# A linear-attention and expert kernel on one core: first scores, warm-up turns, range flag, gate sums and last product rearranged

## Chip, core and metric

The kernel runs on one core of a Trainium2 chip, as one program. The metric is the device time in microseconds of that program. Before the change it is 401.42 us (median of three runs, 400.92 to 402.02).

## What is computed

The reference has two parts. The first is a recurrence over 768 times for 4 batches and 8 heads of 48 dimensions:

```python
cur = np.einsum('bhd,bhe->bhde', u[None] * kt, vt)
y[:, :, t] = np.einsum('bhd,bhde->bhe', rt, state + cur)
state = w[None, :, :, None] * state + np.einsum('bhd,bhe->bhde', kt, vt)
```

Its result, as 3072 rows of 384, goes through a two-level choice of expert: argmax over 4 groups, then argmax over 4 experts of that group, both with softmax weights. Each row passes one expert:

```python
h = np.maximum(xg[mask_e] @ w1[g, e], 0.0)
ye = h @ w2[g, e]
out[tok_idx] = combined[:, None] * ye
```

with w1 of 384x1024 and w2 of 1024x384 for each of the 16 experts.

## The kernel before, in words

The order of the work on every engine is written out by hand: each engine carries out its instructions in the order of the source, and waits at an instruction until what it needs is there.

**Recurrence (lines 274 to 1014).** The 768 times are cut into chunks of 128; with 4 batches this gives NT = 24 chunks, one for each step s of the loop at line 860. For chunk n, `turn` (505) transposes the keys and the queries of the chunk on TensorE (PE): `turn(n, "kT")` into the bank TR, `turn(n, "rT")` into RW; `turn_out` (515) copies kT on ScalarE (ACT) and multiplies rT by the powers `pw` of the decay on VectorE (DVE). `scores(n)` (524) multiplies kT by rT into the two banks of PA, four pairs of heads by two. For every chunk but the first it does so in quarters: the rows 0 to 63 of a 128x128 block against all 128 columns, the rows 64 to 127 against the last 64; the lower left quarter is not needed. `mask(n)` (542) copies the part above the diagonal into `am` on DVE. The diagonal itself comes from `sum_own` (495, DVE, over products `dg` of GpSimd, POOL), `diagonal_here` (553, DVE, five heads) and `diagonal` (558, ACT, the others; those of the list `waiting` run in the next step). `values(n)` (579) multiplies the values by `am` into YB, `state(n)` (567) adds what the state gives, `update(n)` (588) writes the chunk's contribution to the state into columns of the bank MS, from which `carry(n)` (599, DVE) makes the new state R. `values_out(n)` (610) copies YB to `yT` on ACT, `rows_out(n)` (626) turns it into rows.

**Gates.** `gate_parts(n)` (614) multiplies the four quarters of yT by the gate weights into 128 columns of a bank and copies them to `lT` on ACT (three buffers). The bank is MS or TR (line 279), in alternation for n below 7, TR from then on. `gate_sum(n)` (643) adds the four quarters by a matmul with `sel`, into other columns of MS. The parts of chunks 0 and 1 are made in step 3, those of 2 and 3 in step 4, 4 in step 5, 5 and 6 in step 6, then one a step; their sums come a step later, ahead of that step's parts (lines 942 to 950). Four chunks make a turn of the routing (`route_1` to `route_5`), which writes rows to their expert's region by indirect DMA on POOL.

**Range flag.** The decay is held within limits; if any value was outside, a slow path at the end recomputes all. `out_of_range` (751) compares on DVE in step 0, `all_out_of_range` (755) sums over partitions by a matmul into a column of MS, `in_range` (758) makes `not_ok`, and `go_on` (761) a whole number of it, in step 8. `count(12)` (685), in step 14, sums the experts' counts in the same way.

**Start (lines 419 to 840).** `turn_nothing` (420) transposes the identity on PE, with no use of the result: 13 times at the start, 2 after the product that spreads u over the partitions (425), 2 after `mask(0)` and 4 before `turn(1, "kT")`. `WL` and `wl` (828) are the last powers of the decay.

**Experts (1016 to 1166).** 15 slots of up to 212 rows and at the end one of 96 run one after the other: `up` into four banks, `down` by 128 columns with the weights as the stationary side. The two small slots (88 and 96 rows) and the rows done ahead use `rows_down` (238): eight products of 384 columns with the rows as the stationary side, one multiplication by the gate on ACT, one indirect DMA of rows of 384. The slot of 96 rows comes last. `tokens` (252) makes the list of its row numbers on DVE.

Banks: PA and YB are tiles of two banks, TR, RW, MS and SB of one.

Of the kernel before, what the change touches and what calls it, by code (L numbers as in the profile page):

```python
# [29 lines left out]
def kernel(  # L30
# [88 lines left out]
    tagA = [cst([P, 2], f"tagA_{i}") for i in range(4)]  # L119
    idA = [cst([P, 1], f"idA_{i}", I32) for i in range(4)]  # L120
    okA = [cst([P, 1], f"okA_{i}", I32) for i in range(4)]
    cnt_s = cst([P, GE], "cnt_s")
# [128 lines left out]

    def tokens(i, n, count):
        nc.vector.memset(idA[i][0:n], NOWHERE)
        nc.vector.tensor_scalar(
            out=tagA[i][0:n, 0:1].bitcast(I32), in0=tagA[i][0:n, 0:1].bitcast(I32), scalar1=2, scalar2=None,
            op0=OP.logical_shift_right,
        )
        nc.vector.tensor_scalar(out=okA[i][0:n], in0=prow[0:n], scalar1=count[0:n], scalar2=None, op0=OP.is_lt)
        nc.vector.copy_predicated(idA[i][0:n], okA[i][0:n], tagA[i][0:n, 0:1].bitcast(I32))

# [13 lines left out]
    with ExitStack() as rec:  # L274
# [3 lines left out]
        rows_ps = YB[:, :, 2 * P : 4 * P]  # L278
        lT_at = (MS[:, 0:P], TR[:, 0, :])

        spare_at = [0]
# [21 lines left out]
        pre_ps = MS[:, 400 : 400 + 4 * GE]  # L303
        cnt_ps = MS[:, 464 : 464 + GE]

        def scratch(shape, i):
# [67 lines left out]

        nc.vector.memset(y_ps, 0.0)
        nc.vector.memset(padded(rp[0]), 0.0)
        nc.vector.memset(padded(rp[NRP - 1]), 0.0)
# [47 lines left out]
        nc.tensor.matmul(u_ps_all, lhsT=ones[0:1, :], rhs=u_row, start=True, stop=True, skip_group_check=True)  # L425
        turn_nothing(2)
        gates_in()
# [96 lines left out]
        def scores(n):  # L524
            kT, rT = rkT.pop((n, "kT")), rkT[n, "rT"]
            for hc in range(HC):
                for e in range(2):
                    rows = slice(DP * e, DP * e + D)
                    if n == 0:
                        nc.tensor.matmul(  # L530
                            PA[:, e, P * hc : P * (hc + 1)], lhsT=kT[rows, hc, :], rhs=rT[rows, hc, :],
                            start=True, stop=True, skip_group_check=True,
                        )
                        continue
                    for z in range(2):
                        nc.tensor.matmul(  # L536
                            PA[64 * z : 64 * (z + 1), e, P * hc + 64 * z : P * (hc + 1)],
                            lhsT=kT[rows, hc, 64 * z : 64 * (z + 1)], rhs=rT[rows, hc, 64 * z : P],
                            start=True, stop=True, skip_group_check=True,
                        )  # L540
# [72 lines left out]

        def gate_parts(n):
            yT = yTs[n]
            lT_ps = lT_at[n % 2 if n < 7 else 1]
            for q in range(NQ):
                e, j = q // 2, q % 2
                nc.tensor.matmul(  # L619
                    lT_ps[32 * q : 32 * (q + 1), :], lhsT=gwp[:, 4 * j + e, :], rhs=yT[:, e, j, :],  # L620
                    start=True, stop=True, skip_group_check=True,
                )
            lT = mid[n] = pool.tile([P, P], FP32, tag="lT", bufs=3, name="lT")
            nc.scalar.copy(lT, lT_ps)
# [60 lines left out]
        def count(n):  # L685
            nc.tensor.matmul(cnt_ps, lhsT=ones, rhs=cum[:, n, :], start=True, stop=True, skip_group_check=True)

        def keys():
            key = tl([P, GE], "keys")
            nc.vector.scalar_tensor_tensor(  # L690
                out=key, in0=cnt_ps, scalar=float(GE), in1=bias16, op0=OP.mult, op1=OP.add
            )
            return key
# [57 lines left out]
        def out_of_range():  # L751
            nc.vector.tensor_tensor(out=same, in0=wcol, in1=wraw, op=OP.not_equal)
            nc.vector.reduce_max(out=same[:, 0:1], in_=same, axis=AX)

        def all_out_of_range():
            nc.tensor.matmul(cnt_ps[:, 0:1], lhsT=ones, rhs=same[:, 0:1], start=True, stop=True, skip_group_check=True)

        def in_range():
            nc.vector.tensor_scalar(out=not_ok, in0=cnt_ps[:, 0:1], scalar1=0.5, scalar2=None, op0=OP.is_gt)

# [66 lines left out]
        scores(0)  # L827
        nc.vector.tensor_mul(WL, pw[:, :, P // 2], pw[:, :, P // 2])
        nc.scalar.copy(wl, WL)
        for t in am[2:4]:  # L830
            nc.scalar.copy(diagonals(t)[:, 0:HERE], spread(nothing.to_broadcast([P, P]), 1, HERE))
        mask(0)
        turn_nothing(2)
        turn(1, "rT")
        turn_nothing(4, TR)
        turn(1, "kT")
# [23 lines left out]
        for s in range(NT):  # L860
# [44 lines left out]
            if s > CLOSE:  # L905
                update(s)
            values_out(s)
            if s == 0:
                own_term(1)
                out_of_range()  # L910
            for n, e, hc in waiting:
                diagonal(n, e, hc, hc + 1)
            waiting.clear()
            if s <= CLOSE:
                scores(s + 1)
                update(s)
                if s == CLOSE:
                    sum_own(s + 3)
                mask(s + 1)
# [5 lines left out]
            if far < NT:  # L925
                turn(far, "kT")
                turn(far, "rT")
            if s == 0:
                all_out_of_range()
                in_range()  # L930
            if whole:
# [7 lines left out]
            for c in range(NB - 1):  # L939
                if s == first(c) + 1:  # L940
                    route_e(c)
            for n in {4: (0, 1), 5: (2, 3), 6: (4,), 7: (5, 6)}.get(s, (s - 1,) if s > 7 else ()):
                gate_sum(n)
            for c in range(NB - 1):
                if s == first(c) + 2:
                    route_p(c)
                    if c == 2:
                        count(12)
            for n in {3: (0, 1), 4: (2, 3), 5: (4,), 6: (5, 6)}.get(s, (s,) if s > 6 else ()):
                gate_parts(n)  # L950
            if s < CLOSE:
                own_term(far)
            for c in range(NB - 1):
# [4 lines left out]
                if s == first(c) + 2:  # L958
                    if c == 2:
                        key = keys()  # L960
                    route_3(c)
                if s == first(c) + (2 if c >= NB - 3 else 3):
# [18 lines left out]
            if s == CLOSE - 1:  # L981
                turn(s + 3, "kT")
                turn(s + 3, "rT")
                own_term(s + 3)
            if whole:
                diagonal(far, 1)
            if s >= CLOSE and s + 4 < NT:
                sum_own(s + 4)
            if s == 8:
                go_on()  # L990
        for job in late:
# [24 lines left out]
    with ExitStack() as moe:  # L1016
# [55 lines left out]
        def columns(p):  # L1072
# [4 lines left out]
            if s < 2:  # L1077
                tokens(2 + s, SLOTS[s], cnt_s[:, s : s + 1])
                return
# [62 lines left out]
        for p in range(GE):  # L1142
# [10 lines left out]
            if order[p] < 2:  # L1153
                i = order[p]
                po = next_of(downs)
                yt = pool.tile([P, DM], FP32, tag="yd", name="yd")
                rows_down(hTs[p], held(p)[1], 2 + i, SLOTS[i], po, yt)
            else:
                down(p, 0)
# [280 lines left out]
```

## Time and profile before

| what | us |
|---|---|
| median of three runs | 401.42 |
| the profiled execution | 402.09 |
| its span in the profile | 400.3 |
| PE busy | 388.7 (97%) |
| ACT busy | 180.4 (45%) |
| POOL busy | 201.0 (50%) |
| DVE busy | 153.4 (38%) |
| recurrence, up to the last chunk's values | 0 to 128.4 |
| experts, from the first large slot to the last matmul | 162 to 393.1 |

Durations are those of the profiled execution, whose span begins with the first instruction. A row of the timeline gives start, busy time, engine, line of the kernel, operation, written and read tiles (written first), number of instructions, and in brackets how long the engine had been idle and what ended that. PE is the matmul itself, PEld the loading of its stationary side, which stands in the queue ahead of it. An idle engine costs time only where the chain runs through it.

### The profile page before, as it was taken

How to read it: one execution, taken by the hardware profiler on the slowest of the kernel's cores; microseconds unless marked ns; L12 is line 12 of the kernel's file. 1: busy time of each engine (PE TensorE's matmuls, PEld its weight loads, DVE VectorE, ACT ScalarE, POOL GpSimd, SP SyncE). 2: the span in 40 equal slices, each digit the busy share in tenths (PEclk: the TensorE clock that was granted, in tenths of full speed). 3: DMA queues.
4: the chain of work that ended last, by engine and by line, in shares of the span. 5: the costliest groups of instructions: out<-in, count | busy, mean ns of one | idle time of the engine just before them, and what ended most of it. 6: DMA issues, size and time to landing. Idle time of an engine off the chain costs nothing.

```text
span 400.3 us, 10467 instructions
## 1 busy us (share of the span) xinstructions
PE 388.7 (97%) x3963; PEld 361.9 (90%) x3963; DVE 153.4 (38%) x405; ACT 180.4 (45%) x429; POOL 201.0 (50%) x265
## 2 busy tenths in 40 slices
PE   8999999999999999999999999999999999999992
PEld 6787899999888977899999999999999999999981
DVE  7887988888867602101202112111121221211110
ACT  4665888888875211432433424424244244244210
POOL 7999956999842412105162351532624524523542
PEclk9999999999999999999999999999999999999999
DMA  8998999995965977999999999999989999981000
GB/s 159 160 174 159 197 208 221 212 195 147 264 200 123 308 193 212 233 275 258 232 258 243 228 250 266 224 253 284 200 240 259 255 247 268 233 236 28 27 18 27
DMA packets 123118, 81.80 MB, mean 204 GB/s; under 512 B 96863, under 2 KB 114289, under 8 KB 123061
## 3 DMA queue, kind: packets, MB, share of 16 engines
q1 hardware_dynamic: 116019, 71.12, 77.1%
q0 software_dynamic: 4752, 9.55, 8.1%
q8 instruction: 32, 0.52, 0.6%
q10 hardware_dynamic: 2290, 0.40, 0.5%
q14 instruction: 25, 0.20, 0.2%
HBM read 69.89 MB, written 11.67 MB: 204 GB/s over the span
## 4 chain that ended last, share of the span: by engine, by line
issue 46%; PE 29%; POOL 18%; SPq 3%; DVE 2%; DMA 1%; POOLq 1%; ACT 0%
POOL out_dram L1128 16%; PE YB L583 6%; PE PA L536 6%; SPq L323 3%; PE TR L511 3%; PE YB L574 2%; PE YB L630 2%; PE RW L511 2%; PE MS L594 2%; PE TR L619 2%; PE MS L644 1%; DMA vt<-in_v_dram 1%; POOL out_dram L245 1%; PE TR L793 1%; DVE am L543 1%
## 5 line engine op out<-in xcount | busy, mean ns | idle before, releaser
L1128 POOL DMA_INDIRECT out_dram<-yt,idn x93 | 90.4, 972 | 137.1 <-DVE yt L1126 107.0
L1076 DVE STREAM_TRANSPOSE xe<-xg 128x672 f32<-128x672 f32 (+2 forms) x16 | 12.7, 796 | 121.0 <-DMA xg<-x_sorted 88.7
L1116 PE MATMUL YB<-hT,w2p 128*128 128x208 f32 (+10 forms) x336 | 58.7, 328 | 0.0
L1116 PE MATMUL PA<-hT,w2p 128*128 128x208 f32 (+10 forms) x336 | 58.1, 326 | 0.0
L1116 PEld LDWEIGHTS YB<-hT,w2p 128*128 128x128 f32 x336 | 55.8, 190 | 0.0
L1116 PEld LDWEIGHTS PA<-hT,w2p 128*128 128x128 f32 x336 | 55.3, 190 | 0.0
L561 ACT ACTIVATE am<-ident,du 128x128 f32<-128x128 f32 x152 | 50.5, 398 | 0.0
L1125 DVE STREAM_TRANSPOSE yt<-yT 128x672 f32<-128x672 f32 (+1 forms) x14 | 11.8, 842 | 80.4 <-ACT yT L1119 80.4
L1094 ACT COPY w2p<-w 128x1024 f32<-128x1024 f32 x42 | 41.1, 1045 | 3.0 <-DMA w<-in_moe_w_dram 3.0
L543 DVE COPY_PREDICATED am<-later,PA 128x1024 f32<-128x1024 int32 x24 | 31.7, 1323 | 10.8 <-PE PA L536 6.1
L1104 PE MATMUL MS<-xe,w 128*128 128x208 f32 (+12 forms) x192 | 32.8, 320 | 0.0
L1104 PE MATMUL TR<-xe,w 128*128 128x208 f32 (+12 forms) x192 | 32.8, 320 | 0.0
L1104 PE MATMUL RW<-xe,w 128*128 128x208 f32 (+12 forms) x192 | 32.8, 320 | 0.0
L1104 PE MATMUL SB<-xe,w 128*128 128x208 f32 (+12 forms) x192 | 32.7, 320 | 0.0
L1104 PEld LDWEIGHTS SB<-xe,w 128*128 128x128 f32 x192 | 30.8, 190 | 0.6 <-issue 0.2
L1104 PEld LDWEIGHTS MS<-xe,w 128*128 128x128 f32 x192 | 30.7, 190 | 0.0
L1104 PEld LDWEIGHTS RW<-xe,w 128*128 128x128 f32 x192 | 30.7, 190 | 0.0
L1104 PEld LDWEIGHTS TR<-xe,w 128*128 128x128 f32 x192 | 30.7, 190 | 0.0
L230 POOL DMA_INDIRECT x_sorted<-xt,place_i x16 | 16.1, 1003 | 23.6 <-DVE end L719 11.8
L536 PE MATMUL PA<-rT,kT 48*64 48x128 f32 (+1 forms) x736 | 25.6, 255 | 0.5 <-issue 0.5
L583 PE MATMUL YB<-am,vt 128*48 128x128 f32 x384 | 25.9, 277 | 0.1
L490 POOL TENSOR_TENSOR dg<-dg,ub 128x384 f32<-128x384 f32 x24 | 24.1, 1003 | 1.9
(220 smaller groups left out, 560.1 us busy)
## 6 DMA issues: line engine op xcount, KB each, us to landing
w<-in_moe_w_dram SPq DMA_DIRECT2D x128, 384.0 KB, 9.5
vt<-in_v_dram SPq DMA_DIRECT2D x24, 192.0 KB, 4.5
rp<-in_r_dram SPq DMA_DIRECT2D x23, 192.0 KB, 4.3
kt<-in_k_dram SPq DMA_DIRECT2D x22, 192.0 KB, 5.2
xg<-x_sorted SPq DMA_DIRECT2D x36, 85.8 KB, 10.3
x_sorted<-zeros SPq DMA_DIRECT2D x4, 392.0 KB, 4.7
out_dram<-yt,idn POOLq DMA_INDIRECT x93, 7.5
xg<-x_sorted SPq DMA_DIRECT2D x20, 73.5 KB, 8.9
```

The costliest lines, as they stand in the source:

```text
L230: ins = nc.gpsimd.indirect_dma_start(out=xs_dram, out_offset=bass.IndirectOffsetOnAxis(ap=place_i[:, i : i + 1], axis=0), in_=xt[:, i].rea ...
L490: nc.gpsimd.tensor_mul(dg, dg, ub)
L511: nc.tensor.transpose(ps[:, hc, :], two, ident)
L536: nc.tensor.matmul(PA[64 * z : 64 * (z + 1), e, P * hc + 64 * z : P * (hc + 1)], lhsT=kT[rows, hc, 64 * z : 64 * (z + 1)], rhs=rT[rows, hc ...
L543: nc.vector.copy_predicated(am[n % NAM], later.unsqueeze(1).unsqueeze(1).to_broadcast([P, 2, HC, P]).bitcast(I32), PA.rearrange("p e (h t) ...
L561: nc.scalar.mul(am[n % NAM][:, e, hc, :], ident, dus[n][:, i : i + 1])
L583: nc.tensor.matmul(y_at(e, hc), lhsT=vt[:, n % 2, 2 * hc + e, :], rhs=amn[:, e, hc, :], start=(n < 4 and hc < 2), stop=True, skip_group_ch ...
L1076: nc.vector.transpose(xe[:, :, 0:nb, :], xg[:, 0:nb, 0:QW].rearrange("p i (ko a) -> p ko i a", a=32))
L1094: nc.scalar.copy(o4[:, kk], v4[:, kk])
L1104: nc.tensor.matmul(ph[:, i, 0:n], lhsT=w1[:, ko, P * (f + i) : P * (f + i + 1)], rhs=xe[:, ko].rearrange("p i b -> p (i b)")[:, 0:n], star ...
L1116: nc.tensor.matmul(po[:, 0:n], lhsT=w2p[:, d, fo, :], rhs=hT[:, fo, 0:n], start=(fo == 0), stop=(fo == FO - 1))
L1128: ins = nc.gpsimd.indirect_dma_start(out=out_q, out_offset=bass.IndirectOffsetOnAxis(ap=idn[:, i : i + 1].bitcast(U32), axis=0), in_=yt[:, ...
```

## The change

- `scores(0)` is made in quarters like the others; the part of PA that it leaves is set to zero once by DVE at the start.
- The turns of nothing after the spread of u (2), after `mask(0)` (2) and before `turn(1, "kT")` (4) go. `WL` and `wl` come behind `mask(0)`.
- `out_of_range` moves from step 0 to the end of step 8, and writes into a free column of `cum`; its sum over partitions is made as a 17th column of `count(12)` in step 14, `in_range` follows `keys` there, `go_on` moves to step 17.
- `gate_parts` always writes into TR: the first part of a step at columns 0 to 127, the second at 128 to 255. Up to step 5 the sums come behind the parts.
- `turn(7, "kT")`, in step 4, goes to the first bank of PA instead of TR. In step 4 the copy `values_out` comes behind the waiting diagonals.
- The last slot's product is made in two halves of 192 columns, each with a multiplication on ACT and an indirect DMA of its own; `tokens` makes two lists for it.

```diff
+        nc.vector.memset(PA.rearrange("p e (h z t) -> p e h z t", z=2, t=64)[64:P, :, :, 0, :].rearrange("p e h t -> p (e h) t"), 0.0)
...
         nc.tensor.matmul(u_ps_all, lhsT=ones[0:1, :], rhs=u_row, start=True, stop=True, skip_group_check=True)
-        turn_nothing(2)
         gates_in()
...
-                    if n == 0:
-                        nc.tensor.matmul(
-                            PA[:, e, P * hc : P * (hc + 1)], lhsT=kT[rows, hc, :], rhs=rT[rows, hc, :],
-                            start=True, stop=True, skip_group_check=True,
-                        )
-                        continue
...
-        def gate_parts(n):
+        def gate_parts(n, at=0):
             yT = yTs[n]
-            lT_ps = lT_at[n % 2 if n < 7 else 1]
+            lT_ps = TR[:, at, :]
...
+        def count_and_range(n):
+            both = cum[:, n : n + 2, :].rearrange("p i e -> p (i e)")[:, 0 : GE + 1]
+            nc.tensor.matmul(
+                MS[:, 464 : 464 + GE + 1], lhsT=ones, rhs=both, start=True, stop=True, skip_group_check=True
+            )
...
-        nc.vector.tensor_mul(WL, pw[:, :, P // 2], pw[:, :, P // 2])
-        nc.scalar.copy(wl, WL)
...
         mask(0)
-        turn_nothing(2)
+        nc.vector.tensor_mul(WL, pw[:, :, P // 2], pw[:, :, P // 2])
+        nc.scalar.copy(wl, WL)
         turn(1, "rT")
-        turn_nothing(4, TR)
         turn(1, "kT")
...
-            values_out(s)
+            if s != CLOSE - 1:
+                values_out(s)
             if s == 0:
                 own_term(1)
-                out_of_range()
             for n, e, hc in waiting:
                 diagonal(n, e, hc, hc + 1)
             waiting.clear()
+            if s == CLOSE - 1:
+                values_out(s)
...
-            if s == 0:
-                all_out_of_range()
-                in_range()
...
-            for n in {4: (0, 1), 5: (2, 3), 6: (4,), 7: (5, 6)}.get(s, (s - 1,) if s > 7 else ()):
-                gate_sum(n)
+            summed = {4: (0, 1), 5: (2, 3), 6: (4,), 7: (5, 6)}.get(s, (s - 1,) if s > 7 else ())
+            if s > CLOSE:
+                for n in summed:
+                    gate_sum(n)
...
-                        count(12)
-            for n in {3: (0, 1), 4: (2, 3), 5: (4,), 6: (5, 6)}.get(s, (s,) if s > 6 else ()):
-                gate_parts(n)
+                        count_and_range(12)
+            for at, n in enumerate({3: (0, 1), 4: (2, 3), 5: (4,), 6: (5, 6)}.get(s, (s,) if s > 6 else ())):
+                gate_parts(n, at)
+            if s <= CLOSE:
+                for n in summed:
+                    gate_sum(n)
...
             if s == CLOSE - 1:
-                turn(s + 3, "kT")
+                turn(s + 3, "kT", PA[:, 0].rearrange("p (h t) -> p h t", t=P))
...
             if s == 8:
+                out_of_range()
+            if s == 17:
                 go_on()
...
+                if p == last:
+                    for z in range(2):
+                        yt = pool.tile([P, DM // 2], FP32, tag="yh", name="yh")
+                        half_down(hTs[p], held(p)[1], 2 + i, SLOTS[i], z, next_of(downs), yt)
```

The new function for the halves:

```python
    def half_down(hT, w2, i, n, z, po, yt):
        cols = slice(DM // 2 * z, DM // 2 * (z + 1))
        for fo in range(FO):
            nc.tensor.matmul(
                po[0:n, 0 : DM // 2], lhsT=hT[:, fo, 0:n], rhs=w2[:, fo, cols], start=(fo == 0), stop=(fo == FO - 1),
                skip_group_check=True,
            )
        nc.scalar.mul(yt[0:n], po[0:n, 0 : DM // 2], tagA[i][0:n, 1:2])
        ins = nc.gpsimd.indirect_dma_start(
            out=out.rearrange("n (z w) -> (n z) w", z=2),
            out_offset=bass.IndirectOffsetOnAxis(ap=idH[z][0:n].bitcast(U32), axis=0),
            in_=yt[0:n], in_offset=None, bounds_check=2 * N - 1, oob_is_err=False,
        )
```

## The prediction

> **What bounds the kernel.** I read the page first (its table of slices has PE at 8 or 9 tenths everywhere but the last slice), then PE's waits by window, then the timeline of the stretches that the change touches. From 44 to 140 us the waits view gives PE no wait for another engine above 0.2 us, and the chain runs from matmul to matmul; in the expert stage (140 to 393 us) PE has no listed wait at all. So a microsecond that PE gains or loses before 50 us goes to the end unchanged, and little else counts. I call a pass of the loop over s "step s", and part(n) what gate_parts(n) issues.
>
> The start, in the timeline of 0 to 32 us:
>
> ```profile
> 5.96 0.69 PE L422 MATMUL RW<-ident 128*128 128x128 f32 x2
> 6.45 1.06 PE L511 MATMUL MS<-ident,rp 128*128 128x128 f32 x4
> 7.94 0.87 PEld L815 LDWEIGHTS YB<-ident,iw 128*128 128x128 f32 x4
> 10.50 0.47 PEld L511 LDWEIGHTS RW<-ident,rp 128*128 128x128 f32 x4
> ...
> 10.76 1.32 DVE L543 COPY_PREDICATED am<-later,PA 128x1024 f32<-128x1024 int32 x1
> ...
> 14.93 1.32 DVE L543 COPY_PREDICATED am<-later,PA 128x1024 f32<-128x1024 int32 x1
> 16.15 0.34 DVE L604 TENSOR_TENSOR R<-MS,wl 128x192 f32<-128x192 f32 x1
> 16.54 0.30 PEld L756 LDWEIGHTS MS<-same,ones 128*128 128x128 f32 x2 [0.83 <-DVE R L604]
> 16.86 0.82 PEld L583 LDWEIGHTS YB<-am,vt 128*48 128x48 f32 x16
> ```
>
> Two things are to be seen. A turn costs 0.87/4 = 0.22 us until 8.8 us and 0.47/4 = 0.12 after 10.3: PE's clock is released in between. And the matmul of the range flag (L756) holds PE 0.83 us, though it reads nothing of R: it waits because R's multiply reads the same bank MS, at other columns.
>
> The two places with two parts in one step, from the timelines of 28 to 35 and 32 to 60 us:
>
> ```profile
> 28.72 0.59 ACT L520 COPY kT<-TR 128x512 f32<-128x512 f32 x1
> ...
> 29.31 0.19 PEld L619 LDWEIGHTS MS<-yT,gwp 128*32 128x32 f32 x8 [0.48 <-issue]
> 29.45 0.26 PEld L619 LDWEIGHTS TR<-yT,gwp 128*32 128x32 f32 x8
> ```
>
> ```profile
> 47.42 0.16 PEld L619 LDWEIGHTS TR<-yT,gwp 128*32 128x32 f32 x8
> 47.56 0.24 PEld L619 LDWEIGHTS MS<-yT,gwp 128*32 128x32 f32 x8
> ...
> 48.00 0.85 PEld L536 LDWEIGHTS PA<-rT,kT 48*64 48x64 f32 x32 [0.20 <-issue]
> ...
> 48.62 0.26 ACT L662 ACTIVATE ex<-ex 128x80 f32<-128x80 f32 x1
> ...
> 48.78 0.25 ACT L624 COPY lT<-TR 128x128 f32<-128x128 f32 x1
> ```
>
> The second part follows the first at 0.14 us because it goes to another bank; ACT fetches the first one much later (48.78).
>
> The end, in the timeline of 375 to 401 us:
>
> ```profile
> 387.81 5.33 PE L240 MATMUL YB<-w,hT 128*96 128x384 f32 x16
> 391.30 0.97 POOL L1128 DMA_INDIRECT out_dram<-yt,idn  x1 [0.31 <-issue]
> 393.18 0.58 ACT L244 ACTIVATE yd<-YB,tagA 96x384 f32<-96x384 f32 x1 [4.83 <-PE YB L240]
> 394.03 0.94 POOL L245 DMA_INDIRECT out_dram<-yd,idA  x1 [1.76 <-ACTq L1170]
> ```
>
> **Part by part.** Sums are against the profiled execution: span 400.3, time 402.09, which is 0.67 above the median of 401.42.
>
> *Warm-up turns.* The two turns at 5.96 stand right before turn(0, rT), whose four follow back to back (6.45), so its data are there; without them it starts at 5.97, and turn_first and the iw turns, queued behind, 0.48 earlier too. T2's copy on ACT follows (9.25 to 8.77), and with it POOL's row of 1.0 us operations that starts at 9.81. The scores start at 8.73 instead of 9.20, and run at the slow clock up to the release, so they end near 10.1 instead of 10.4. The other six turns (10.33, 10.94) end on no path: PE waits for the mask until 12.14 anyway. The new memset of half of PA is taken at the 0.48 us of the memset of 128x512 (L375); DVE has a wait of 0.58 us for wraw ahead of 3.19, which covers it. Without that cover it would cost at most those 0.48.
>
> *Quarters and WL.* 32 matmul passes instead of 16; the quarters of later steps take 1.10 us (L536), the whole ones 1.16 (L530): nothing. mask(0) now waits for the scores, for ACT's three diagonals (0.98 us, starting after the sum of du near 9.1) and no longer for WL (0.34): 10.2 instead of 10.76. WL and wl fall behind it, and kT(1)'s copy on ACT behind wl, at about 12.0 instead of 12.19; scores(1) then start near 12.7 (13.15). mask(1) waits for ACT's diagonals of step 1, behind the first yT copy: 14.2 instead of 14.93.
>
> *Range flag.* Its two DVE operations ahead of mask(1) go (their end at 15.02 set its start as much as the diagonals' at 14.76), and L756 leaves PE. Values(1) then wait for mask(1) alone: 14.2 + 1.32 + 0.06 = 15.55 instead of 16.86. **Head: -1.3.** What is late next: du(2) needs POOL's dg, 16.85 before and 16.4 now, used at 17.08 before; it fits, and from there mask, values, yT copy and diagonals form a ring of 4.06 us a step (values from 16.86 to 20.92) which starts 1.3 earlier. Where the turns bring nothing (the release falls earlier in that run), only the flag's part is left: mask(1) at 14.80, behind the diagonals' end at 14.76, then values(1) at 16.2, 0.65 earlier. Bounds -0.6 and -1.4. The flag's DVE work at step 8 (0.65) and 14 (0.14) stands in a DVE that is idle some 15% there and is followed by masks due a step later; a 17th column in the count (0.18 us for 16): nothing. If that cover were gone, 0.8.
>
> *Parts in TR.* Part(1), (3) and (6) now go to the bank from which ACT still has to copy part(0), (2), (5). L756 above and L644 at 34.81 (0.27 behind DVE's ts, other columns of MS) show that a matmul into a bank waits for the reader of other columns of it, and I find no matmul in the timeline that starts into one of these tiles while ACT or DVE reads it. The rows show it for DVE; that ACT's copies count as well is an inference. The Trainium skill's page "PSUM — Partial Sum Buffer", section "PSUM bank collisions raise a hardware error", says that accesses have to be kept apart by bank and 32-partition quadrant, not by address, for ScalarE too; by it the sum is the one below, and if addresses alone counted it would be the first rival's.
> Step 3: part(0) waits for kT's copy (28.72 + 0.59 = 29.31, as before for R), its lT copy runs 29.84 to 30.11, part(1) starts at 30.15 instead of 29.45, and behind it on PE stand state(4) and values(4), with every later matmul. **+0.65.**
> Step 4: parts first, on TR behind kT's copy (34.81): 34.86, copy to 35.61, part(3) 35.65, sums 35.87 (0.52), state 36.6, then turn(7, kT), which in PA no longer waits for lT (36.84 before): 36.95. Values(5) at 37.85 against 37.84. The diagonals ahead of the yT copy let mask(5) start 0.4 earlier, but nothing of PE waits for it now. **0**, bounds -0.45 and +0.3. ACT's lT(3) waits for sum(0) in its buffer, 0.2 us behind part(3): hidden.
> Step 5: part(4) fills the 0.43 in which the sums waited for ts (42.09): **-0.2**.
> Step 6: ACT has the copy of part(5) at 48.78, behind rows, diagonals and exp; it ends at 49.03, part(6) starts at 49.08 instead of 47.56. Scores(8), state(7) and values(7) stand behind it. **+1.5**; 0 if no wait comes.
>
> *Last product.* 32 passes of 192 columns instead of 16 of 384: 0.32 a pass becomes 0.16 (the 164-column passes of L1116 take 0.14, weights included), PE ends alike. ACT's last copy covers 192 columns: 0.33 as L1109 at 128x192, not 0.58. POOL's first half runs in its idle time (its last L1128 ends at 392.27; 392.57 to 393.51); the second starts 0.30 behind it or 0.27 behind ACT, 393.8 instead of 394.03. **-0.2.** The landing takes 3.6 us for 96 rows of 1536 bytes and 2.2 for L1128's 49 KB, so up to -1.6 if the end waits for it; I keep the nearer row, the same instruction's, since half is still 96 rows. The few more DVE operations of the last tokens() lie in a DVE idle for 10.95 us. No edit moves a DMA of SP's queue; POOL's gets this one more.
>
> **Sum:** -1.3 + 0.65 + 0 - 0.2 + 1.5 - 0.2 = +0.45: 402.09 becomes 402.5, the median 401.42 becomes **401.8**.
>
> **Rivals.** *No wait by bank for ACT's copies* (faster): step 3 then costs 0.05, step 6 nothing, step 4 gains 0.4: -1.3 + 0.05 - 0.4 - 0.2 - 0.2 = -2.05, 399.4. For it speaks only that no row shows an ACT reader of other columns; against it L756 and L644.
> *Fewer turns release the clock later* (slower): from 5.96 to 9.2 PE is as busy as before, since the gap only moves from 8.95 to 8.5; that speaks against. Price: slow scores(0), twice the 1.0 of L530, end at 8.73 + 2.0 = 10.75 instead of 10.1 (+0.65); if the release is later than 12.2, values(0) double as well (+1.0). +1.65 in all: 403.4. It decides from a release about 3 us late. The skill's page "TensorE: Matmul & The Clock Gate", section "The HAM clock gate", has the clock released after some 3.4 us of sustained work in a free-running window: one window late would be this case; its section on PE-mode transpose says turns hardly count as busy, while here the clock is released after a stretch of turns.
> *The head gives half* (the turns' data or the release differ from run to run; the three times spread by 1.1): -0.65 instead of -1.3, 402.4.
>
> **How the numbers follow.** Forecast 0.50, its own range 400.9 to 402.7; half a head 0.18; no wait 0.17; late clock 0.15. A measurement of this kernel tells about 0.3%, 1.2 us. Faster by more: no wait 0.17 and 0.03 of the forecast (a landing that counts): 0.20. Slower: late clock 0.15 and 0.07 of half a head: 0.22. Same: 0.58. The range takes in the no-wait and late-clock cases at their centres, 399.3 to 403.4.
>
> **What would show it.** Values(1) at 15.5 instead of 16.86; part(1) about 0.7 behind part(0); at step 6 a PE gap of 1.5 us ended by ACT's lT; POOL's last DMA 1.0 to 1.3 after the one before. Without that gap the forecast is wrong towards 399.4; turns of 0.22 us after 10 us would make it wrong the other way.

## The result, and the profile after

The kernel before took 401.19 us (median of 22 runs, 399.65 to 406.95), the changed one 401.48 us (22 runs, 400.83 to 407.85). The ratio is **1.0017, with a 95% interval of 1.0003 to 1.0032**: 0.1 to 1.3 us slower, forecast 401.8 against 401.42. The profiled execution of the changed kernel is the longest of its 22: PE waits in it for gathered rows in the expert stage (3.9 us ahead of the matmuls of L1128), where the profile of before has no such wait, and the ratio leaves it out; so it is read here up to the expert stage and in its last slot, not by its end.

The start of the changed kernel, in the timeline of 5 to 17 us:

```profile
6.74 1.00 POOL L511 TENSOR_TENSOR dg<-rp,rp 128x384 f32<-128x384 f32 x1 [0.32 <-DMA rp<-in_k_dram]
8.78 0.95 PEld L552 LDWEIGHTS PA<-rT,kT 48*64 48x64 f32 x32 [0.39 <-issue]
...
9.44 0.99 ACT L577 ACTIVATE am<-ident,du 128x128 f32<-128x128 f32 x3
...
10.46 1.35 DVE L559 COPY_PREDICATED am<-later,PA 128x1024 f32<-128x1024 int32 x1
11.68 0.79 DVE L850 TENSOR_TENSOR SB<-pw 128x4 f32<-128x4 f32 x1
...
16.07 0.83 PEld L599 LDWEIGHTS YB<-am,vt 128*48 128x48 f32 x16 [0.49 <-DVE am L559]
```

The last row is values(1): 16.07 instead of 16.86. In the first row POOL's dg waits 0.32 us for a load, and the sum du, ACT's diagonals and mask(0), which follow one from the other, come later than forecast. The multiplication for WL, behind mask(0) now, takes 0.79 us (0.34 before).

The two steps with a second part, in the timelines of 28 to 32 and 46 to 52 us:

```profile
28.65 0.19 PEld L635 LDWEIGHTS TR<-yT,gwp 128*32 128x32 f32 x8 [0.55 <-issue]
29.16 0.27 ACT L640 COPY lT<-TR 128x128 f32<-128x128 f32 x1 [0.58 <-PE TR L635]
29.48 0.16 PEld L635 LDWEIGHTS TR<-yT,gwp 128*32 128x32 f32 x8 [0.64 <-ACT lT L640]
```

```profile
47.47 0.16 PEld L635 LDWEIGHTS TR<-yT,gwp 128*32 128x32 f32 x8
...
48.82 0.25 ACT L640 COPY lT<-TR 128x128 f32<-128x128 f32 x1
49.12 0.16 PEld L635 LDWEIGHTS TR<-yT,gwp 128*32 128x32 f32 x8 [1.50 <-ACT lT L640]
```

Before, the second part followed the first by 0.14 us. Now it starts 0.05 us behind the end of ACT's copy of the first, out of other columns of TR: the loading of weights stands still for 0.64 us in step 3 and 1.50 in step 6.

The end, in the timeline of 385 to 407 us:

```profile
399.60 0.42 ACT L260 ACTIVATE yh<-PA,tagA 96x192 f32<-96x192 f32 x1 [2.18 <-PE PA L256]
400.29 0.92 POOL L261 DMA_INDIRECT out_dram<-yh,idH  x1 [0.40 <-ACTq L1198]
```

From the last slot's first matmul (382.49 before, 388.87 after) to the end of the span it took 17.81 us and now takes 17.13. Of the 0.68, 0.14 are won up to the end of POOL's last DMA instruction; 0.54 are won behind it, where the span ends 4.79 us later instead of 5.33.

**Where the time went.** The position of values(n) in the timeline holds all that PE lost before it. The table gives it for values(1), (4), (5), (6) and (7), with the profiled executions of the experiments to follow; the step lengths in it are differences of neighbours.

| kernel | v(1) | v(4) | v(5) | v(6) | v(7) | step 4: v(5)-v(4) | step 5 | step 6 |
|---|---|---|---|---|---|---|---|---|
| before | 16.86 | 30.50 | 37.84 | 44.46 | 49.46 | 7.34 | 6.62 | 5.00 |
| changed | 16.07 | 30.42 | 38.10 | 44.51 | 50.94 | 7.68 | 6.41 | 6.43 |
| a_two_banks | 16.21 | 29.98 | 37.58 | 44.34 | 49.34 | 7.60 | 6.76 | 5.00 |
| b_parts_tr | 16.87 | 31.15 | 38.80 | 45.42 | 51.85 | 7.65 | 6.62 | 6.43 |
| c_head | 15.76 | 29.45 | 36.63 | 44.62 | 49.62 | 7.18 | 7.99 | 5.00 |
| d_halves | 17.21 | 30.94 | 38.30 | 44.97 | 49.97 | 7.36 | 6.67 | 5.00 |
| k_shift | 16.96 | 30.68 | 38.04 | 44.88 | 49.88 | 7.36 | 6.84 | 5.00 |
| j_align | 15.51 | 29.81 | 37.49 | 43.86 | 50.29 | 7.68 | 6.37 | 6.43 |
| l_two_aligned | 16.19 | 29.90 | 37.50 | 43.87 | 48.87 | 7.60 | 6.37 | 5.00 |
| m_wl_aligned | 15.58 | 29.30 | 36.90 | 43.27 | 48.27 | 7.60 | 6.37 | 5.00 |
| p_best | 16.02 | 29.61 | 36.26 | 42.63 | 47.63 | 6.65 | 6.37 | 5.00 |
| q_pool64 | 16.77 | 30.44 | 37.80 | 44.43 | 49.43 | 7.36 | 6.63 | 5.00 |
| r_128 | 16.72 | 30.36 | 37.69 | 44.80 | 49.80 | 7.33 | 7.11 | 5.00 |
| t_two_turns | 16.06 | 29.64 | 36.29 | 42.66 | 47.66 | 6.65 | 6.37 | 5.00 |

So the change won 0.79 us in the head, lost 0.71 by values(4), 0.34 in step 4 and 1.43 in step 6, and won 0.21 in step 5: +1.48 at values(7). With 0.68 won at the end that is +0.8; the ratio gives +0.7.

That the two agree does not show that the 1.48 us reach the end. They stand unchanged up to values(18) (99.14 before, 100.63 after). Behind it PE stands still twice in the profile of before, for nothing that the profile shows (0.75 us ahead of 103.83, 0.89 ahead of 110.69), and in the other it does not: at values(23) the changed kernel is 0.38 ahead (126.98 against 127.36). One execution of each cannot tell which of this belongs to the kernels.

### The profile page after: what moved, and what is told of

It reads as the page before. It is cut to its first block, busy times and chain, and to the rows that moved or that the text cites. A ratio compares the mean times of both kernels' runs of the same rounds, so it can differ in the third digit from the quotient of the medians.

```text
span 406.0 us, 10518 instructions
## 1 busy us (share of the span) xinstructions
PE 389.7 (96%) x3985; PEld 364.3 (90%) x3985; DVE 154.5 (38%) x409; ACT 181.3 (45%) x430; POOL 202.1 (50%) x266
## 4 chain that ended last, share of the span: by engine, by line
issue 47%; PE 28%; POOL 18%; DVE 2%; ACT 1%; DMA 1%; POOLq 1%; ACTq 0%; DVEq 0%
POOL out_dram L1152 16%; PE YB L599 6%; PE PA L552 5%; PE TR L533 3%; PE YB L590 2%; PE YB L646 2%; PE TR L635 2%; PE RW L533 2%; PE MS L610 2%; DMA rp<-in_k_dram 1%; PE MS L660 1%; POOL out_dram L246 1%; PE TR L812 1%; DVE am L559 1%; ACT am L577 1%
## 5 line engine op out<-in xcount | busy, mean ns | idle before, releaser
L1128 PE MATMUL SB<-xe,w 128*128 128x208 f32 (+12 forms) x192 | 33.9, 328 | 3.9 <-DVE xe L1100 3.9
L1128 PEld LDWEIGHTS SB<-xe,w 128*128 128x128 f32 x192 | 31.5, 195 | 5.1 <-DVE xe L1100 4.5
L1128 PE MATMUL MS<-xe,w 128*128 128x208 f32 (+12 forms) x192 | 33.5, 325 | 0.0
L1128 PE MATMUL TR<-xe,w 128*128 128x208 f32 (+12 forms) x192 | 32.8, 320 | 0.0
L1128 PE MATMUL RW<-xe,w 128*128 128x208 f32 (+12 forms) x192 | 32.8, 320 | 0.0
L1128 PEld LDWEIGHTS MS<-xe,w 128*128 128x128 f32 x192 | 31.5, 195 | 0.0
L1128 PEld LDWEIGHTS RW<-xe,w 128*128 128x128 f32 x192 | 30.7, 190 | 0.0
L1128 PEld LDWEIGHTS TR<-xe,w 128*128 128x128 f32 x192 | 30.7, 190 | 0.0
L552 PEld LDWEIGHTS PA<-rT,kT 48*64 48x64 f32 x768 | 20.6, 133 | 5.0 <-issue 4.1
```

The costliest lines, as they stand in the source:

```text
L552: nc.tensor.matmul(PA[64 * z : 64 * (z + 1), e, P * hc + 64 * z : P * (hc + 1)], lhsT=kT[rows, hc, 64 * z : 64 * (z + 1)], rhs=rT[rows, hc ...
L1128: nc.tensor.matmul(ph[:, i, 0:n], lhsT=w1[:, ko, P * (f + i) : P * (f + i + 1)], rhs=xe[:, ko].rearrange("p i b -> p (i b)")[:, 0:n], star ...
```

## The experiments

The theory: a matmul into a bank waits until ACT's copy out of other columns of that bank has ended, and this is what the change pays; the rest is the head, worth less than forecast. The rival: ACT's late copy is only where PE's wait is put down, and another wait would stand there without it. TR and MS are tiles of one bank each, so "bank" and "tile" say the same here, and no run tells them apart.

One thing sets how the runs are read. On the chips that these kernels ran on, the kernel before itself took 413.5 to 440.4 us. From about 100 us on PE waits, and its granted clock is lower: from 100 to 140 us it is busy for 34.6 of the 40 us at a clock of 0.87 in a_two_banks, against 38.8 at 1.00 in the profile of before. Executions of one kernel differ by 6 to 19 us. Differences of 1 or 2 us are not to be read from such ends. The steps up to 50 us are steadier: step 6 takes 5.00 or 6.43 us in all fourteen traces. So the positions of values(n) decide; only values(1) moves by 0.5 to 0.7 us with the moment at which PE's pace rises (runs 6 and 7), and each kernel has one trace. The ratios to the kernel before are given all the same.

**1. Two banks (a_two_banks).** The edit against the changed kernel:

```diff
-            lT_ps = TR[:, at, :]
+            lT_ps = MS[:, 0:P] if at else TR[:, 0, :]
...
-            lT = mid[n] = pool.tile([P, P], FP32, tag="lT", bufs=3, name="lT")
+            lT = mid[n] = pool.tile([P, P], FP32, tag="lT", bufs=4, name="lT")
```

> The changed kernel with the second part of a step written to MS again (and a fourth buffer for lT, without which sum(0) and lT(3) would wait for each other); all else as changed. Theory (a matmul that writes TR waits for ACT's copy out of other columns of TR): the waits of 0.66 us ahead of part(1) and part(3) and of 1.50 us ahead of part(6) go. Step 3 gives back 0.65, step 4 about 0.35 to 0.7, step 6 1.44: values(7) start at 48.1 to 48.6 us instead of 50.95, and the time falls by about 2.5 us against the changed kernel, 0.6%, to 1.8 us or 0.45% under the kernel before: about 399.4. Rival 1 (ACT is late with rows, diagonals and exp, and something else behind the parts, the scores or the state, needs it just as late): values(7) stay at 50 or later, and the time within 0.2% of the kernel before. Rival 2 (the gain comes, but is given back in the expert stage, which would be bound by its loads): values(7) near 48.4 and the end of the span unchanged.

Its timeline of 46 to 53 us:

```profile
47.31 0.16 PEld L635 LDWEIGHTS TR<-yT,gwp 128*32 128x32 f32 x8
47.44 0.24 PEld L635 LDWEIGHTS MS<-yT,gwp 128*32 128x32 f32 x8
```

The second part follows after 0.13 us, and step 6 is back at 5.00. The waits of 0.64 and 1.50 us are gone and nothing took their place in steps 3 and 6, against rival 1; but step 4 stays at 7.60, and values(7) come 1.60 us ahead of the changed kernel, not 2.4 to 2.8. The ratio for the whole is 1.0188 (1.0133 to 1.0243). That is slower, against the expectation and against the lead at values(7); it came about behind 100 us, and what of it belongs to this kernel is not settled.

**2. Only the bank (b_parts_tr).** The kernel before with

```diff
-            lT_ps = lT_at[n % 2 if n < 7 else 1]
+            lT_ps = TR[:, at, :]
```

(and the loop over the parts counts `at`, as in the diff of the change).

> The kernel before with one edit of the change alone: all parts are written to TR, the second of a step to other columns of the same bank; sums still stand ahead of the parts, warm-up, flag and last product as before. Theory (one bank, one wait): part(1) stands about 0.65 us later than now behind part(0), part(6) about 1.5 behind part(5), step 4 between 0 and 0.4: +2.2 to +2.6 us, 0.55 to 0.65%, about 403.5. Rival (the waits seen in the changed kernel come from the sums having moved behind the parts, or from ACT being earlier or later through the head): within 0.2% of the kernel before, and no gap of over 0.5 us ahead of part(6).

Its timeline of 46 to 53 us:

```profile
48.38 0.16 PEld L619 LDWEIGHTS TR<-yT,gwp 128*32 128x32 f32 x8
50.03 0.16 PEld L619 LDWEIGHTS TR<-yT,gwp 128*32 128x32 f32 x8 [1.50 <-ACT lT L624]
```

The same 1.50 us, in a kernel whose sums stand ahead of the parts and whose head is the old one; values(4) +0.65, step 4 +0.31, step 6 +1.43, values(7) +2.39, inside the expected 2.2 to 2.6. The theory holds, the rival falls. Ratio 1.0124 (1.0038 to 1.0210).

**3. Only the head (c_head).** The kernel before with quarters, memset, no turns of nothing, WL behind mask(0) and the flag counted with the tiles; `idH`, the two lists for the halves (the diff above leaves their declaration out), is declared in it, but not used. Of that diff it takes the hunks on PA's memset, `turn_nothing`, `scores`, `WL` and the flag; the sums and parts stay:

```diff
+            for n in summed:
+                gate_sum(n)
...
             for n in {3: (0, 1), 4: (2, 3), 5: (4,), 6: (5, 6)}.get(s, (s,) if s > 6 else ()):
                 gate_parts(n)
```

> The kernel before with the head's edits alone: first scores in quarters, half of PA set to zero, fewer turns, WL behind mask(0), the range flag counted with the tiles. Theory (the head is worth what the changed kernel's trace shows, 0.8 us, since mask(0) starts only 0.3 earlier and WL takes 0.79 beside POOL's operation): values(1) at 16.0 to 16.2 us instead of 16.86, and every later step as far ahead: -0.8 us, -0.2%, about 400.4. Rival (the head's gain is lost at the steps 2 to 5, where another engine is late): values(1) at 16.1, but values(5) at 37.8 as now, and the time as before. Rival (the forecast's head was right and the other edits took from it): values(1) near 15.5 and -1.3 us.

Values(1) at 15.76 and values(5) at 36.63: 1.1 to 1.2 us ahead, more than the changed kernel's 0.8 (PE's pace rose before 5.6 us in this execution, see run 6), and then step 5 takes 7.99 us instead of 6.62, behind a wait of 1.87 us of the turns for POOL's kp. POOL is late because it waited 3.15 us, until 30.9, for a load of rp, a wait that the kernel before does not have. So the head's gain was lost at step 5, but to a load that no instruction of the head issues or moves (runs 5 to 7 follow it). Ratio 1.0145 (1.0063 to 1.0228).

**4. Only the halves (d_halves).** The kernel before with the last product in halves, and `tokens` for it:

```diff
+                if p == last:
+                    for z in range(2):
+                        yt = pool.tile([P, DM // 2], FP32, tag="yh", name="yh")
+                        half_down(hTs[p], held(p)[1], 2 + i, SLOTS[i], z, next_of(downs), yt)
```

> The kernel before with the last product in halves alone. Theory (the second half's copy and POOL's issue end 0.15 to 0.2 us earlier, and half as many bytes land sooner): counted from the last slot's first matmul, POOL's last DMA ends 0.15 us earlier and the span ends another 0.45 us earlier: -0.6 us, -0.15%, about 400.6. Rival 1 (only POOL's issue counts, the landing does not shrink): -0.2 us, which this measurement can hardly tell from nothing. Rival 2 (32 passes of 192 columns cost PE more than 16 of 384, the loads of weights no longer hidden): the last slot's product takes longer than the 5.33 us that the 16 passes took, and the time rises by up to 0.5 us.

From the last slot's first matmul to the end it took 17.84 us, against 17.66 to 18.07 in the kernels here with the whole product: no gain can be seen. What lies behind POOL's last DMA instruction is shorter, 3.91 us against 5.01 to 5.19, but that instruction comes 1.1 to 1.5 us later, behind a later copy by ACT. The 16 matmul passes more cost nothing that shows. No ratio can be given: its executions took 424.2 to 440.4 us, those of the kernel before 425.4 to 439.2. What stood out was at the other end: it, too, waits 3.19 us for rp at step 4 and loses 0.5 us by values(7), though the edit is in the last slot.

**What the four have in common.** The runs 1, 3 and 4 and the changed kernel declare `idH`, 64 bytes among the constants; the kernel before and run 2 do not. In the first group rows of 192 bytes (the trace's DMA packets of that size) take 22.9 to 24.4 ns in SP's queue between 4 and 12 us, in the second 16.0 to 16.7. The next three runs follow this.

**5. 64 bytes and nothing else (k_shift).** The kernel before with

```diff
     idA = [cst([P, 1], f"idA_{i}", I32) for i in range(4)]
+    pad = cst([P, 16], "pad")
```

> The kernel before with one more constant tile of 64 bytes, which nothing reads or writes: every tile allocated behind it stands 64 bytes further on in each partition, as it does in the changed kernel through idH. Theory (where the tiles stand sets how long a row of 192 bytes takes): packets of 192 bytes take about 25 ns instead of 15 between 4 and 18 us, as in the changed kernel, the head alone and the halves alone; POOL waits for rp ahead of dg twice, 0.4 to 0.9 us near 20 and 2.6 to 3.2 us near 28; values(7) start at 49.8 to 50.0 us instead of 49.46, as in the halves alone, and the time rises by 0.3 to 0.5 us, 0.1%, or more where the memory is slow. Rival (the slow rows come from the run, the chip or the program's instructions): 15 to 17 ns throughout and values(7) at 49.4 to 49.5.

**6. The place put back (j_align).** The changed kernel with

```diff
     idH = [cst([P, 1], f"idH_{z}", I32) for z in range(2)]
+    pad = cst([P, 112], "pad")
```

> The changed kernel with an unused constant tile of 448 bytes behind idH, so that every tile behind it stands 512 bytes from where it stands in the kernel before, instead of 64. Theory (place of the tiles): packets of 192 bytes take 15 to 17 ns from the start, dg(0) begins at 6.4 us instead of 6.74, mask(0) at 10.1 to 10.2 instead of 10.46, values(1) at 15.7 to 15.8 instead of 16.07, and POOL waits for no rp at step 4; values(7) at about 50.6 and the time 0.3 us (0.1%) less than the changed kernel's. Rival (place does not count): packets of 25 ns, values(1) at 16.1, the same time as the changed kernel.

One line of the table by windows for each: busy time (and instructions) of PE, PEld, DVE, ACT and POOL, then clock, DMA share and GB/s. The kernel before:

```profile
6.00:8.00 2.00, 2.00 (x11) 2.00 (x11) 1.13 (x4) 1.93 (x6) 1.92 (x3) 1.00 1.21 230
```

k_shift:

```profile
6.00:8.00 2.00, 1.15 (x9) 0.86 (x8) 1.73 (x5) 1.31 (x5) 1.40 (x2) 1.00 1.52 167
```

j_align:

```profile
6.00:8.00 2.00, 1.25 (x9) 0.78 (x8) 1.93 (x5) 1.94 (x6) 1.92 (x3) 1.00 1.30 243
```

With 64 unused bytes the DMA engines are busier (1.52 against 1.21) and move less: 167 against 230 GB/s, 27.6 ns a row against 16.0. Values(7) come at 49.88, as in the halves alone. With 512 bytes the changed kernel loads at 243 GB/s, POOL's dg starts at 6.39, mask(0) at 10.12 and values(1) at 15.51: 1.35 us ahead of the kernel before, where the forecast had 1.3. The gain of 0.56 at values(1) is larger than the 0.3 expected, and not all of it is the place: in this execution four turns take 0.42 us from 5.4 us on (an early clock), in the profile of the changed kernel 0.87 us until 8.4 and 0.42 only from 9.9 (a late one). Runs 7, 9 and 12 have the same place and a late clock. Ratios for runs 5 and 6: 1.0177 (0.9922 to 1.0432) and 1.0103 (0.9735 to 1.0471).

**7. Two banks and the place (l_two_aligned).** Runs 1 and 6 together.

> Second part of a step in MS again (and the fourth lT buffer), with the tiles placed as in the kernel before. Theory (one bank, one wait; and the place of the tiles): values(1) at 15.7 to 15.8, no wait for ACT's lT ahead of part(1), (3) and (6), no wait of the turns for kp at step 5; values(7) at 48.5 to 48.8 us instead of 49.46, and with the tail's 0.5 the time 1.2 to 1.5 us under the kernel before, 0.3 to 0.4%. Rival (step 4 keeps 0.25 whatever the banks, since the sums now stand behind the parts): values(5) follow values(4) by 7.6 instead of 7.34, and values(7) at 48.7 to 48.8. Rival (place does not count): values(7) at 49.3, as with the two banks alone.

No wait for kp at step 5 any more (6.37), values(7) at 48.87. But values(1) stand at 16.19, no earlier than in the changed kernel (16.07), with a late clock: the weights of the scores, started at 8.78, take 1.61 us (0.89 in run 6), and in the timeline of 8 to 16 us mask(0) waits for them:

```profile
10.78 1.32 DVE L560 COPY_PREDICATED am<-later,PA 128x1024 f32<-128x1024 int32 x1 [0.74 <-PE PA L553]
```

Step 4 stays at 7.60, as the first rival has it. Its timeline of 31.5 to 38.5 us shows why:

```profile
34.97 0.27 ACT L641 COPY lT<-MS 128x128 f32<-128x128 f32 x1
...
35.34 0.52 PEld L661 LDWEIGHTS MS<-sel,lT 128*128 128x128 f32 x4 [0.72 <-POOL zeros L898]
35.38 0.59 PE L661 MATMUL MS<-sel,lT 128*128 128x20 f32 x4 [0.48 <-ACT lT L641]
```

The sums write MS, out of which ACT copies lT(3) until 35.24, and they start 0.1 behind it; the matmul's row names ACT's lT. They read lT(0) and lT(1), which had long been there. It is the same wait, moved from the part to the sums. Ratio 1.0132 (1.0052 to 1.0212), again slower by the end.

**8. WL early (m_wl_aligned).** Run 7 with

```diff
+        nc.vector.tensor_mul(WL, pw[:, :, P // 2], pw[:, :, P // 2])
+        nc.scalar.copy(wl, WL)
         own(0, 0)
```

(and the two lines behind `mask(0)` go).

> The kernel of the run before this one, with WL's multiply put ahead of mask(0) again, directly behind T2's chain, where DVE waits for du anyway. Theory (behind mask(0) WL takes 0.79 us because it ends only with POOL's operation beside it, and kT(1)'s copy, scores(1), the diagonals of step 1 and mask(1) all stand behind that): mask(1) and values(1) 0.4 earlier, values(1) at 15.3 to 15.4 us, and everything behind as much: 0.4 us or 0.1% less than without. Rival 1 (mask(1) is set by POOL's dg(1) through du and the diagonals, not by WL): values(1) as without. Rival 2 (ahead of mask(0) WL meets a POOL operation too and holds du(0) and so mask(0) back): mask(0) at 10.4 or later, values(1) no earlier.

Values(1) at 15.58, no earlier than the 15.51 of run 6, where WL stands behind mask(0) and takes 0.18 us. Rival 1 is nearest: values(1) follow values(0) by 4.03 in both (both with an early clock), set by the yT copy and the diagonals on ACT. Behind mask(0) WL took 0.17 to 0.89 us in the kernels here; only where it took 0.79 (changed kernel) and 0.89 (run 9) are values(1) later, 4.21 and 4.29 behind values(0). So it costs 0.2 to 0.3 in some executions, not the 0.4 expected. Ratio 1.0034 (0.9918 to 1.0150).

**9. The best version (p_best).** Run 6 with

```diff
-            lT_ps = TR[:, at, :]
+            lT_ps = MS[:, 0:P] if n in (0, 2, 6) else TR[:, at, :]
...
-            if s > CLOSE:
+            if s > CLOSE or s == 4:
...
-            if s <= CLOSE:
+            if s <= CLOSE and s != 4:
```

> The changed kernel with what the runs so far ask for: tiles placed as in the kernel before (the 448 bytes), part(0), part(2) and part(6) in MS so that no step has both of its parts in one bank, and the sums of step 4 ahead of its parts again (behind them at step 5, where it gained 0.25). Theory (step 4 pays 0.3 for either, the sums behind the parts or the shared bank, as 7.64, 7.61 and 7.68 us from values(4) to values(5) against 7.34 say): values(5) follow values(4) by 7.3 to 7.4 us, values(6) by 6.4, values(7) by 5.0, and values(7) start at 47.9 us where the clock is released before 5.4 us, at 48.6 where it is released near 9: 0.9 to 1.5 us ahead of the kernel before; with the tail's 0.5, the time 1.4 to 2.0 us or 0.35 to 0.5% below it. Rival (step 4's 0.3 comes from turn(7, kT) in PA, which all of them but the kernel before and the parts alone have): 7.6 at step 4 here too, and values(7) at 48.2 to 48.9.

Its timeline of 31.5 to 38.5 us:

```profile
33.52 0.52 PEld L661 LDWEIGHTS MS<-sel,lT 128*128 128x128 f32 x4
...
34.08 0.16 PEld L636 LDWEIGHTS MS<-yT,gwp 128*32 128x32 f32 x8
34.21 0.24 PEld L636 LDWEIGHTS TR<-yT,gwp 128*32 128x32 f32 x8
```

Sums, part, part, without a wait. Step 4 takes 6.65 us, 0.69 less than before and more than the theory had. Of this, 0.40 lie ahead of the sums: they start 3.91 us behind values(4) instead of 4.31 and no longer wait for DVE's ts, which follows mask(5). In the eight kernels with values_out behind the diagonals mask(5) starts 2.23 to 2.24 us behind values(4), in the six others 2.63 to 2.64. The other 0.29 lie between the sums and values(5) (2.74 us instead of 3.03), where turn(7, kT) in PA no longer waits for lT: a gain, not the cost that the rival saw in it. Values(7) at 47.63, 1.83 ahead of the kernel before. The end does not show it: 429.87 against 432.56 us, with executions from 417.7 to 436.5, and no ratio. Part of the lead is lost again at the end: from the last slot's first matmul it takes 18.87 us, against 17.81 in the profile of the kernel before. The same 18.8 to 19.0 stand in the runs 6, 7, 8 and 12, all with the 448 bytes and the halves; ACT's last copy there starts 2.1 to 2.3 us behind the end of the last load of weights, in the changed kernel 0.36. Why is open. That this version beats both kernels is thus shown up to 70 us only.

**10 and 11. Which place (q_pool64, r_128).** The kernel before with 64 bytes in the pool ahead of vt, and with 128 bytes among the constants.

```diff
+        pad = pool.tile([P, 16], FP32, tag="pad", bufs=1, name="pad")
         raw[0, "v"] = load(v, 0, "vt", 4)
```

> The kernel before with 64 unused bytes ahead of vt's buffers instead of among the constants: vt, kt, rT, kT, dg and what is allocated behind them stand 64 bytes further on, while rp, kp, am and the constants stay. Theory (the place of the tiles that a load fills sets its packets' time): the packets of vt and kt take 20 to 26 ns between 6 and 10 us as in the kernel with 64 bytes among the constants, those of rp 15 to 17. Rival (rp's place alone counts, and the others' packets only share its delay): 15 to 17 ns for all. Rival (the place of another tile counts, one that an engine works on meanwhile): 25 ns for rp as well, or 15 for all.

> The kernel before with an unused constant tile of 128 bytes instead of 64. By the runs so far 64 bytes make packets of 192 bytes take 25 ns between 4 and 18 us, and 512 bytes leave them at 15. If the place counts by a multiple of 128 bytes, 15 to 17 ns here; if by 256 or 512, 20 to 26 ns.

With vt, kt and all behind them moved, and rp not: 16.3 ns a row from 6 to 8 us. With 128 bytes among the constants: 26.7 ns, values(7) at 49.80. So the tiles that are not in the pool count (rp, kp, am and others), neither 64 nor 128 bytes will do, and by run 11's expectation the place counts by 256 or 512 bytes. The times: 434.06 and 431.78 us, one execution each.

**12. Two turns put back (t_two_turns).** Run 9 with

```diff
+        turn_nothing(2)
         gates_in()
```

> The kernel of the run before last (two banks, step 4's sums first, tiles placed as before) with the first two warm-up turns put back. The records show the release of PE's clock in two places from run to run: before 5.4 us, or between 9 and 10 us, with and without those turns. Theory (in the late case the turns are worth keeping: with them PE starts the scores at 9.20 us and runs them at the full pace, to 10.02, in all four late runs that had them; without them it starts at 8.78 and runs part of them at half pace, to between 9.6 and 10.2): mask(0) starts at 10.1 to 10.3 and values(0) at 11.4 to 11.6 us in either case, instead of 11.73 to 12.15 in the late one, values(1) at 15.5 to 15.6 and values(7) at 47.1 to 47.2: 0.45 us less than 47.63, 0.1% of the time. Rival (the late release waits for nothing that the turns do, and falls anywhere from 9 to 10): turns of 0.22 us up to 8.4, scores from 9.20 that end later than 10.3, values(0) at 12.1 or later, values(7) at 48.0.

The weights of the first scores start at 9.21 and take 0.94 us: the scores do run at the full pace, as the theory has it. But mask(0) starts at 10.65 and not at 10.1 to 10.3: rT, kT and the sum du, on DVE behind the turns, are 0.4 us later too, and ACT's diagonals, which it waits for, with them. Values(1) at 16.06 and values(7) at 47.66 against 16.02 and 47.63: in this pair, both with a late clock, the turns neither help nor hurt. Theory and rival both miss. Ratio 1.0045 (0.9991 to 1.0100).

## Why the prediction was right, point by point

- **Sum.** Forecast +0.45 against the median (401.87; the prediction writes 401.8), measured +0.7 (0.1 to 1.3). The case called likeliest came, and its large term was right: **step 6, +1.5**, measured 1.43 with a gap of 1.50 ended by ACT's lT; **step 3, +0.65**, measured 0.71; **step 5, -0.2**, measured -0.21. That ACT's copies out of other columns count was called an inference; runs 1, 2, 7 and 9 show it, with and without the rest of the change. Luck had a part: the head and step 4 fell short by 0.51 and 0.34, and the end made up 0.48 of that. And the premise that what PE loses before 50 us goes to the end unchanged holds up to values(18) in the two profiles, not behind it.
- **Head, -1.3: measured -0.79.** The term "mask(0) at 10.2, mask(1) at 14.2" was mis-sized: 10.46 and 14.64. In that trace dg starts behind a later load of rp, at 6.74 and not at 6.37 as in the kernel before, which makes 0.26 at mask(0). WL at 0.34 behind mask(0) became 0.79, and values(1) follow values(0) by 4.21 instead of 4.03: the next 0.2. "No edit moves a DMA of SP's queue" was true of the queue and wrong about the loads. The place is not the whole reason: the forecast's own numbers (10.12, 14.14, 15.51) appear with the tiles in the old place and an early clock; with that place and a late clock values(1) come at 16.19 and 16.02 (runs 7 and 9), where mask(0) waits for the scores. The forecast let the scores end near 10.1 at a late clock; that was its second weak point.
- **Step 4, 0 with bounds -0.45 and +0.3: measured +0.34.** The wait of part(3) was in the sum; what was short are the rows behind it: part(3) to the sums 0.36 us instead of 0.22, turn(7, kT) to values(5) 1.02 instead of 0.90.
- **End, -0.2: measured -0.68** in the one pair of traces, within the bound named for the landing. The sum left the landing as it was; behind POOL's last DMA instruction it takes 3.91 to 4.81 us in the eight traces with halves and 5.01 to 5.33 in the six without. In run 4, and in all other runs with halves, this is given back by a later copy, so the gain of the whole end is not shown beyond that pair.
- **The turns and the late-clock rival.** PE's pace rises before 5.6 us or between 8.4 and 10.4, in kernels with and without those turns; runs 6 and 7 have the same instructions up to there and fall on either side. Without the turns the weights of the first scores take 0.95, 1.22, 1.46 and 1.61 us in the late case (changed kernel, runs 9, 1 and 7) and 0.89 in the early one; with the turns the late case exceeds the early one by no more than 0.07. So in three of the four the pace rose well into the scores, as the rival has it, and in run 7 its first term came as priced: it put the end of the scores at 10.75, and mask(0) starts at 10.78, values(1) 0.64 behind the forecast's 15.55. Its second term, values(0) at half pace, came nowhere. What the turns would win there they cost in DVE's start (run 12).
- **No wait by bank** is refuted by runs 1 and 2. **Half a head** comes nearest to the measured head (-0.65 for -0.79), and one of its two reasons, a release that differs from run to run, is what the traces show; for the whole time the forecast is nearer.

## What to carry to other kernels

Before two small products share a bank, look at when the reader of the first one runs: if other work stands ahead of it on its engine, the second product and all of PE's queue wait for that work (0.64 us in step 3, 1.50 in step 6). An order that avoids a wait in one place can put it on the next writer of the same bank; follow every writer. A new constant, even an unused one, moves all tiles behind it, so compare the rate of the first loads in both profiles before a change is charged with what its loads do.

## What the runs showed of the hardware

- **The place of a tile sets the rate of its loads.** With 64 or 128 bytes more in front, rows of 192 bytes take 27 to 28 ns from 6 to 8 us instead of 15 to 17, at 166 to 169 instead of 227 to 244 GB/s, in all six kernels that have them in front of rp; with none, with 512, or with 64 behind rp, none of the eight does. The rows of rp lie 256 bytes apart. By the sizes of the tiles in front of it, added up in steps of 32 bytes (an estimate; no trace gives the place), they begin 64 bytes behind a multiple of 256 in the fast kernels, 128 and 192 behind one in the slow ones, where each row crosses a multiple of 256. The Trainium skill's page "DMA: Bandwidth & Descriptors", section "How a descriptor splits into AXI transactions", says of reading that a transfer is cut at multiples of 256 bytes, so that such a row takes two transactions; rp, which is written here, agrees with it from 4 us on. That this is the reason is not shown: the first 1024 rows of SP's queue, which go to rp too, take 15.6 to 17.1 ns in the slow kernels, and the page does not say why the rows of vt, which lie at the same four places modulo 256 in all kernels, take 26 ns as well. 256 bytes were not tried.
- **PE's pace rises at two places.** Four turns take 0.87 us up to 8.4 us in some executions and 0.42 from 5.3 us on in others, while the granted clock in the profile's rows is 1.00 in both.
